# Norm vector folded into two dense weights, more blocks turned by transfers, and a new order of work, in a fused attention and token-mixing kernel

## The chip, the cores and the metric

The kernel runs on one core of a Trainium2 chip. TensorE (PE) multiplies matrices and writes into PSUM; VectorE (DVE) and ScalarE (ACT) compute elementwise and move PSUM to SBUF; GpSimd (POOL) computes elementwise in SBUF and issues the loads; SyncE (SP) issues the stores and the turning transfers. The metric is the device time of one execution in microseconds, as the median of several runs.

## What is computed

```python
kv  = einsum('bhsd,bhse->bhde', k, v)            # 8 batches, 8 heads, 576 tokens, head size 64
o   = einsum('bhsd,bhde->bhse', q, kv)
o   = o / sqrt(mean(o*o, -1) + 1e-6) * g_norm    # g_norm: 64 numbers
x   = o.transpose(0, 2, 1, 3).reshape(8, 576, 512)
theta = x @ w_theta
y   = w_tok_r @ (x*cos(theta)) + w_tok_i @ (x*sin(theta))   # w_tok: 576 x 576, over the tokens
u   = x + y
out = u + maximum(u @ w_ch, 0)
```

All inputs and the output are float32; the kernel computes in fp16 with fp32 sums.

## The kernel before

The 576 tokens of a batch are four full tiles of 128 (j = 0 to 3) and a tail of 64 (j = 4), which is kept with its 512 channels folded onto 128 partitions. For each batch the steps are these; the names are those of the code's tasks, and of the tiles in the profile.

- `ld...`: loads of k, v and q, converted to fp16, from GpSimd's queue.
- `kv`, `ko`: kv of all heads on PE, copied into block-diagonal matrices `kbd` by DVE or ACT.
- `qt`, `qo` or `qd`: the queries turned (transposed). Batches in `TURNED` use a TensorE transpose with an identity and a copy out of PSUM into `qD`; the others use a turning transfer (DMA_TRANSPOSE) from SP into `qDD`, two per batch. The tail always uses TensorE.
- `raw`, `sq`, `ss`, `rt`, `x`: the product with kbd on PE, squares on ACT, row sums on DVE, the power -1/2 on GpSimd, and the scaling on DVE. x is normalized but not yet multiplied by g_norm. One tile `x` holds a pair of token tiles, and both `x` steps of the pair must be done before either is whole.
- `xt`, `xo`: x turned by TensorE into `xps`; the copy out of PSUM multiplies by `gcol` (g_norm along the partitions) and writes `xTb`, of which there are two for all batches (b mod 2).
- `th`, `pt`, `arg`, `abs`, `sin`, `cos`, `z`: theta on PE with `wth`; rounding to whole turns on ACT, the rest on DVE, the absolute value on DVE or ACT, two sines on ACT into `sc`, and the two products with x on DVE into `zm` (tail: `zt`).
- `y`, `ye`: the token mixing on PE, directly in turned form for the full tiles, into `y`.
- `us`: u in turned form on DVE (line 595): y times gcol, plus xTb, into `uTb`. `um`, `ug`, `ute`, `uoe`: the same for the tail, with the factor on GpSimd.
- `ut`, `uo`: u turned back by TensorE into `ups` and copied into `ur`; for batches in `UD` (5 and 6) a turning transfer, `ud`, does it into `urd`.
- `v`, `fin`, `st`: u times `wch` on PE, the maximum and the addition of u on DVE into `ot` (three tiles), and the store on SP.

PSUM has four banks for `acc` (kv, th, y, v), two for `raw` and two for what TensorE turns. SP, like every engine, takes its instructions in order, and one that waits holds those behind it.

Nothing schedules at run time: `plan()` numbers the tasks, and the table `TURNS` is a hand-kept list of these numbers in the order in which they are issued, with a letter where another engine than the planned one takes the step, and with fillers (`f`, `a`, `r`: matmuls on constant data at the start). An engine's program is that list, cut down to its own tasks.

Of the kernel before, what the change touches and what calls it, by code (L numbers as in the profile page):

```python
# [9 lines left out]
FP32 = mybir.dt.float32  # L10
# [8 lines left out]
P = 128  # L19
# [9 lines left out]
NURD = 2  # L29
UD = (5, 6)  # L30
NX, NXE, NUR, NOT, NQD, NQD2 = 4, 3, 3, 3, 4, 4
TURNED = (0, 1)
# [10 lines left out]
def plan():  # L43
# [91 lines left out]
11 17 15 14 0 6 4 1 9 5 2 3 7 8 10 a1 16 f42 51 18 65 f7 43 44 45A 52D 46D f3 53 54 f13 47 48 66 49A  # L135
55 20 f11 58 59D 72 21A 50 f1 60 61 73 12 13 180 177 56 179 178 57 79 67 68 62 80D 69 a1 f8 25 26 63
64 29 70 30A f8 86 22D 87D 71 23A 24 74 37 75 38A 95 76 96D 182 181 77 88 81 33 89 90 82 83 91 34A
452 84 f5 35 31 92 36 93 97 98 78 32D 318 317 320 316 315 319 104 39 105D 85 99 94 100 40 113 327
114 106 27 122 123D 28D 101 107 19 102 115 41 116 108 124 109A 110 125 42A 103 183 184 135 185 217
186 117 118 126 187 127 188D 218 328 119 128 120 111 129 121 134 132 189 196 133 190D 197 191 210  # L140
203 198 112 138 139 130 143 144 192 193 194 140 199 204 211D 200 201 148 195 349 350 145 150 137 205
152 151 714 149 202 206 207 153 131 142 233 224 234 208 448 321 219 322 147 323 481 324 220 326 482D
325A 136 141 225D 209 221 146 222 212 213 214 226 215 223 227 228 229 584 159 447 449 716 450 160
235 164 260 161 166 236 230 261 165 237 216 162 238 163 231 242 251 239 243 252D 262 263 329 167 232
451 253 154 330 240 264 331 244 241 254 155 255 334 169 156 245 613 174 332 581 459 171 335 256A 246
248 257 266 258 336 175 247 157 333 337 712 460 259 158 269 270 273 339 249 250 275 265A 170 267 340
614 338 356 274 268 365 357 279 344 280 345 341 172 284 358 342 453 285 359 366 278 454 283 745 455
343 351 456 360 288 346 367 352 362 347 290 271 353 458D 368 369 370A 457A 173 168 354 746D 291D 348
371 361 363 272 276 383 374 281 277 355 384D 286 364 461 282 392 385 466 287 375 462 393 372 463 289
579 583 964 297 373 302 394 312 464 467 386 468 469 395 298 303 582 376 387 396 313 465 292 294 304  # L150
471 293D 470 488 389 398 397A 377 388A 489 378 305 295 379 580 968 966 842 390 380 399 381 476 299
497 490 391 300 307 382 592 591 296 314 176 306 301 472 308 491 477 401 402 406 473 474 400 492 493A
494 498 478 407 495 479 713 840 411 412 585 405 586 410 416 475 417 587 415 871 588 483 484 589A 499
480 485 872 590D 506 403 486 515 593 496 507D 487 404 500 594 965 598 715 599 516 420 595 501 711
596 408 409 524 502A 503 600 422 525D 423 504 414 413 517 419 418 597 601 838 309 518 519 505 520
602 310 424 439 508 425 509 526 603 426 527 604 440 620 441 608 629 528 621 510 512 311 521 530 723
427 442 511 605 630D 622 429 436 724 443 428 513 514 522 609 534 434 533 523 623 529A 531 610 624
606 532 611 839 837 841 421 539 538 625A 435 430 626 607 437 544 543 717 997 615 718 537 549 612 616
617 548 719 542 720 998 627 849 618 444 547 638 631 721A 722 725 726 632 628 552 554 536 445 619
555D 639D 730 727 633 647 541 640 656 546 553 728 648 731 438 634A 732 729 641 535 850 657 635 735  # L160
733 540 649 736 545 551 642 636 644 734 737 643 761 752 738 550 650 651 753D 645 843 576 844 747 845
658 846 762 748 847A 848 749 739 556 566 431 567 659 557D 637 577 750 740 561 763 432 660 646 652A
741 742 568 558 571 754 764 743 963 967 765 653 654 751 446 433 578 662 661A 562 655 569 570 668 572
788 851 673 744 779 663 789D 559 664 669 790 674 679 755 852 756 758 678 856 853 854 683 573 684 791
780 857 757 792 858 563 855 574 564 859 685 766A 759 781 686 770 767 768 793A 771 794 687 795 860
769 760 976 665 861 670 782 783 772 866 675 667 878 672 862 867 863 560 975 575 864 785 773 784 868
774 680 869 865 666 565 677 671 682 887 676 969 970 873 971 708 776 786 775A 777 681 879 888D 787
# [16 lines left out]
def kernel(  # L184
# [64 lines left out]
    def full(j):  # L249
        return j < NJ  # L250
# [468 lines left out]
```

## Time and profile before

| what | value |
|---|---|
| median of 3 runs | 207.62 us (207.25 to 207.88) |
| the profiled execution | 208.0 us |
| its span, first to last instruction | 206.2 us |
| granted TensorE clock in it | 0.988 |
| busy time PE / DVE / ACT / POOL | 188.1 / 170.7 / 137.2 / 111.1 us |
| bytes moved by DMA | 30.98 MB |

Busy time counts an instruction from start to end; where instructions of an engine overlap, the union is counted. PE's matmuls are pipelined, so a mean of 379 ns for a 512-column matmul is its latency and not the distance to the next one. "Idle before, <- releaser" in a group's row is the time that the engine stood still before these instructions, with what ended it. The chain that ended last is followed back from the last instruction: each piece was released by the one ahead of it.

### The profile page before, as it was taken

To read this page: it belongs to the slowest core of one execution; us is meant where nothing else is said; L and a number is where in the kernel's file an instruction comes from. 1 tells how busy PE (TensorE), PEld (TensorE's weight loads), DVE (VectorE), ACT (ScalarE), POOL (GpSimd) and SP (SyncE) were. 2 spreads that over 40 slices of the span, in tenths; PEclk is the share of its full clock that TensorE was granted. 3 is DMA by queue.
4 is the path that set the end of the run, shared out by engine and by line. 5 is a ranking of instruction groups with operands and counts; after the bars stand their busy time and mean duration, and the time that the engine had idled before them with its cause. 6 is when DMAs were issued, how large, how long until landed. Compare 5 with 4: busy or idle time off the path is not lost.

```text
span 206.2 us, 4614 instructions
## 1 busy us (share of the span) xinstructions
PE 188.1 (91%) x1802; PEld 109.6 (53%) x1802; DVE 170.7 (83%) x346; ACT 137.2 (67%) x276; POOL 111.1 (54%) x112
## 2 busy tenths in 40 slices
PE   0997999999999999999999999979999999999960
PEld 0875766565555555645565756435564554444520
DVE  7036998999999999999998999699998987855560
ACT  2035999369986899767988996959888449500210
POOL 7959984489944985895396534725065320000010
PEclk9999999999999999999999999999999999999995
DMA  5999999999999999899999968919222143236461
GB/s 99 164 197 286 192 190 183 198 164 89 169 189 167 246 184 123 174 155 187 221 151 220 160 154 121 212 24 186 74 105 76 25 80 113 90 77 128 156 244 36
DMA packets 61577, 30.98 MB, mean 150 GB/s; under 512 B 30644, under 2 KB 56884, under 8 KB 61556
## 3 DMA queue, kind: packets, MB, share of 16 engines
q0 software_dynamic: 38864, 16.80, 65.2%
q1 hardware_dynamic: 22692, 13.90, 29.0%
q8 instruction: 14, 0.23, 0.5%
q14 instruction: 7, 0.06, 0.1%
HBM read 33.06 MB, written 9.44 MB: 206 GB/s over the span
## 4 chain that ended last, share of the span: by engine, by line
DVE 34%; PE 32%; DMA 11%; POOL 8%; ACT 6%; issue 6%; DVEq 0%; POOLq 0%
PE y L581 11%; PE th L496 7%; DMA out_dram<-ot 6%; DMA uTb<-in_moe_w_tok_r_dram 5%; DVE zm L556 5%; PE v L496 5%; DVE ot L648 4%; POOL rt L457 4%; DVE uTb L595 4%; DVE ss L451 4%; DVE arg L524 4%; DVE x L469 3%; DVE zt L565 3%; DVE kbd L273 2%; PE xps L388 2%
## 5 line engine op out<-in xcount | busy, mean ns | idle before, releaser
L457 POOL TENSOR_TENSOR rt<-ss,mhalf 128x8 f32<-128x8 f32 x32 | 53.5, 1679 | 44.1 <-DVE ss L451 44.0
L581 PE MATMUL y<-wT,zm 128*128 128x512 f16 x256 | 61.7, 379 | 0.0
L581 PEld LDWEIGHTS <-zm 128*128 128x128 f16 x256 | 23.7, 98 | 24.3 <-issue 0.2
L496 PE MATMUL th<-wth,xTb 128*128 128x512 f16 x128 | 32.7, 379 | 0.1
L496 PE MATMUL v<-wch,uTb 128*128 128x512 f16 x128 | 31.9, 379 | 0.2 <-DVE uTb L595 0.2
L595 DVE SCALAR_TENSOR_TENSOR uTb<-y,gcol,xTb 128x512 f16<-128x512 f32 x32 | 23.2, 741 | 4.4 <-PE y L581 4.4
L269 ACT COPY ur<-ups 128x512 f16<-128x512 f16 x21 | 12.1, 594 | 18.5 <-PE ups L388 18.2
L442 ACT ACTIVATE sqb<-raw 128x512 f32<-128x512 f32 x32 | 19.2, 601 | 7.5 <-PE raw L422 7.4
L469 DVE TENSOR_TENSOR x<-raw,rt 128x512 f16<-128x512 f32 x32 | 21.9, 684 | 2.3 <-POOL rt L457 2.2
L451 DVE TENSOR_REDUCE ss<-sqb 128x8 f32<-128x520 f32 x32 | 21.9, 686 | 2.2 <-ACT sqb L442 1.8
L542 ACT ACTIVATE sc<-arg 128x512 f16<-128x512 f32 x32 | 19.9, 631 | 4.8 <-DVE arg L524 3.9
L548 ACT ACTIVATE sc<-arg,quarter 128x512 f16<-128x512 f32 x32 | 22.8, 724 | 0.1
L524 DVE SCALAR_TENSOR_TENSOR arg<-pt,th 128x512 f32<-128x512 f32 x32 | 21.6, 679 | 1.4 <-ACT pt L519 1.3
L609 POOL TENSOR_TENSOR uge<-ue,g 128x256 f32<-128x256 f16 x8 | 5.4, 673 | 30.5 <-DVE ue L603 30.5
L556 DVE TENSOR_TENSOR zm<-x,sc 128x1024 f16<-128x1024 f16 x32 | 21.5, 681 | 0.1
L519 ACT ACTIVATE pt<-th 128x512 f32<-128x512 f32 x32 | 19.1, 601 | 1.9 <-PE th L496 1.8
L648 DVE SCALAR_TENSOR_TENSOR ot<-v,ur 128x512 f32<-128x512 f32 x24 | 16.1, 681 | 4.5 <-DMA out_dram<-ot 4.0
L496 PEld LDWEIGHTS <-uTb 128*128 128x128 f16 x128 | 11.6, 98 | 11.5 <-issue 0.9
L496 PEld LDWEIGHTS <-xTb 128*128 128x128 f16 x128 | 11.3, 98 | 11.1 <-ACT xTb L271 0.9
L269 ACT CAST kbd<-kv 64x256 f16<-64x256 f32 (+1 forms) x26 | 8.9, 341 | 11.5 <-PE kv L371 11.0
L271 ACT ACTIVATE xTb<-xps,gcol 128x512 f16<-128x512 f16 x20 | 13.6, 684 | 3.5 <-PE xps L388 2.5
L388 PE MATMUL xps<-ident,x 128*128 128x128 f16 x128 | 12.1, 219 | 0.4 <-DVE x L469 0.4
(107 smaller groups left out, 319.5 us busy)
## 6 DMA issues: line engine op xcount, KB each, us to landing
out_dram<-ot SPq DMA_DIRECT2D x32, 256.0 KB, 2.7
k<-in_k_dram POOLq DMA_DIRECT2D x7, 512.0 KB, 11.0
v<-in_v_dram POOLq DMA_DIRECT2D x7, 512.0 KB, 9.1
qh<-in_q_dram POOLq DMA_DIRECT2D x7, 512.0 KB, 10.8
out_dram<-ote SPq DMA_DIRECT2D x8, 128.0 KB
zm<-in_moe_w_theta_dram POOLq DMA_DIRECT2D x1, 768.0 KB, 11.5
uTb<-in_moe_w_tok_r_dram POOLq DMA_DIRECT2D x1, 576.0 KB, 10.3
uTb<-in_moe_w_tok_i_dram POOLq DMA_DIRECT2D x1, 576.0 KB, 12.9
```

What stands on the lines that cost most here:

```text
L269: nc.scalar.copy(out=dst, in_=src)
L451: nc.vector.reduce_sum(out=ss[:], in_=live.pop(("sq", b, j))[:], axis=AXX)
L457: nc.gpsimd.tensor_tensor(out=rt[:], in0=live.pop(("ss", b, j))[:], in1=mhalf[:, 0:h], op=ALU.pow)
L469: nc.vector.tensor_tensor(out=live["xp", b, p][:, :, a * HC:(a + 1) * HC].rearrange("p t (h e) -> p h t e", e=D), in0=r[:].rearrange("p (h ...
L496: nc.tensor.matmul(t[:], lhs(kc), w[:, kc, :], start=(kc == 0), stop=(kc == NKC - 1))
L524: nc.vector.scalar_tensor_tensor(out=arg[:, 0, :], in0=live.pop(("pt", b, j))[:], scalar=MAGIC, in1=live.pop(("th", b, j))[:], op0=ALU.sub ...
L542: nc.scalar.activation(out=sc[:, 1, :], in_=live["arg", b, j][:, 0, :], func=AFT.Sin, bias=0.0, scale=-TURN * SHRINK,)
L548: nc.scalar.activation(out=live["sc", b, j][:, 0, :], in_=live.pop(("arg", b, j))[:, 1, :], func=AFT.Sin, bias=quarter[:], scale=-TURN * S ...
L556: nc.vector.tensor_tensor(out=zm[b % NZ][:, j, :, :], in0=x.unsqueeze(1).broadcast_to((P, 2, C)), in1=sc[:], op=ALU.mult,)
L581: nc.tensor.matmul(t[:], r[:, c * P:(c + 1) * P], wT[:, w, 0:SM], start=(w == 0), stop=(w == 2 * NJ))
L595: nc.vector.scalar_tensor_tensor(out=uTb[:, b % NUT, :, c, :], in0=live.pop(("y", b, c))[:].rearrange("p (j t) -> p j t", j=NJ), scalar=gc ...
L648: nc.vector.scalar_tensor_tensor(out=ot[:], in0=live.pop(("v", b, j))[:], scalar=0.0, in1=u, op0=ALU.max, op1=ALU.add,)
```

## The change

- **The norm vector goes into the weights.** w_theta is scaled row by row with g_norm (it was scaled with a constant in the same step), and w_ch gets a new step `wcs` that scales it in place: three instructions on DVE, one on ACT. So xTb and uTb hold x and u without g_norm: the copies `xo` and `uoe` have no scale any more, and `us` is a plain addition.
- **Where u itself is needed** in the last step, g_norm comes in when u is turned back: `ut` is now an ordinary product with `gdiag`, a diagonal matrix of g_norm, into an fp32 PSUM tile, and `uo` reads fp32.
- **x of batches 5, 6 and 7** (full tiles) is turned by transfers on SP, `xd`, two per batch, straight into xTb. The transposes and copies for them go.
- **u of batches 4, 5 and 6** (before: 5 and 6) is turned back by transfers; since it lacks g_norm, GpSimd multiplies each tile (`um2`, 12 of 128x512, fp32 out, three buffers).
- **Batch 2's queries** are turned by TensorE instead of two transfers.
- **The table `TURNS` is new.** Every line of it differs.

Counted over the program: 48 transposes of x and 16 of u fewer and 16 of queries more on PE; on SP six transfers of x and two of u more and two of queries fewer; 12 products more on GpSimd; full copies of turned x 20 to 13 on ACT and 12 to 7 on DVE.

```diff
-NURD = 2
-UD = (5, 6)
+NURD, NUM2 = 2, 3
+UD = (4, 5, 6)
+XD = (5, 6, 7)
-TURNED = (0, 1)
+TURNED = (0, 1, 2)
...
+    for kc in range(NKC):
+        add("wcs", "DVE", kc)
...
-            add("xt", "PE", b, j)
-            add("xo", "ACT", b, j)
+            if b not in XD or j == NJ:
+                add("xt", "PE", b, j)
+                add("xo", "ACT", b, j)
+            elif j % 2 == 0:
+                add("xd", "SP", b, j // 2)
...
+            if b in UD and j < NJ:
+                add("um2", "POOL", b, j)
...
 TURNS = """
-11 17 15 14 0 6 4 1 9 5 2 3 7 8 10 a1 16 f42 51 18 65 f7 43 44 45A 52D 46D f3 53 54 f13 47 48 66 49A
+8 6 0 9 1 4 5 2 3 17 15 14 16 f28 55 69 20 70D 21 56 7 11 10 r1 83 18 f10 47 48 50D 49A f3 57 58 f17
...
+        nc.vector.tensor_scalar(
+            out=gth[:], in0=gcol[:], scalar1=UNIT / (2.0 * math.pi), scalar2=None, op0=ALU.mult
+        )
+        nc.vector.tensor_scalar(
+            out=gdiag[:], in0=ident[:], scalar1=gcol[:], scalar2=None, op0=ALU.mult
+        )
 
     def e_wth(eng, kc):
-        by = UNIT / (2.0 * math.pi)
-        copy_out(eng, wth[:, kc, :], wth_s[:, kc, :], by)
+        copy_out(eng, wth[:, kc, :], wth_s[:, kc, :], gth[:])
+
+    def e_wcs(eng, kc):
+        copy_out(eng, wch[:, kc, :], wch[:, kc, :], gcol[:])
...
-        copy_out(eng, dst, live.pop(("xp_", b, j))[:], gcol[:])
+        copy_out(eng, dst, live.pop(("xp_", b, j))[:])
+
+    def e_xd(eng, b, p):
+        src = live["xp", b, p][:].rearrange("p t c -> p (t c)")
+        dst = xTb[b % NXT][:, 2 * p:2 * p + 2, :, :].rearrange("p j k c -> p (j k) c")
+        nc.sync.dma_start_transpose(out=dst, in_=src)
...
-        nc.vector.scalar_tensor_tensor(
+        nc.vector.tensor_tensor(
             out=uTb[:, b % NUT, :, c, :],
-            in0=live.pop(("y", b, c))[:].rearrange("p (j t) -> p j t", j=NJ), scalar=gcol[:],
-            in1=xTb[b % NXT][:, :, c, :], op0=ALU.mult, op1=ALU.add,
+            in0=live.pop(("y", b, c))[:].rearrange("p (j t) -> p j t", j=NJ),
+            in1=xTb[b % NXT][:, :, c, :], op=ALU.add,
         )
...
-        copy_out(eng, d[:], live.pop(("up", b, NJ))[:], gcol[:])
+        copy_out(eng, d[:], live.pop(("up", b, NJ))[:])
 
     def e_ut(eng, b, j):
-        turned("ups", lambda i: uTb[:, b % NUT, j, i, :], NKC, ("up", b, j))
+        t = live["up", b, j] = bank([P, NKC, P], FP32, "tr", 2, "ups")
+        for i in range(NKC):
+            nc.tensor.matmul(
+                t[:, i, :], uTb[:, b % NUT, j, i, :], gdiag[:], start=(i == 0), stop=(i == NKC - 1)
+            )
...
+    def e_um2(eng, b, j):
+        u = live["ur", b, j] = wk("um2", [P, C], FP32, NUM2)
+        nc.gpsimd.tensor_tensor(
+            out=u[:].rearrange("p (h e) -> p h e", h=H),
+            in0=live.pop(("ud", b, j)).rearrange("p (h e) -> p h e", h=H),
+            in1=g8[:].unsqueeze(1).broadcast_to((P, H, D)), op=ALU.mult,
+        )
```

Three places show how the instructions move. The first is SP's queue around batch 5. Before, it holds stores (ot full tiles, ote tails) and the turning of batch 6's queries (qDD from qh0):

```order
L654 DMA out_0_dram<-ot_1802 128x512
L654 DMA out_0_dram<-ot_1800 128x512
L412 DMA_TRANSPOSE qDD_1970<-qh0_72 128x8x128
L654 DMA out_0_dram<-ot_1885 128x512
L412 DMA_TRANSPOSE qDD_2071<-qh0_72 128x8x128
L660 DMA out_0_dram<-ote_2018 2x64x256
L654 DMA out_0_dram<-ot_2242 128x512
```

After it, the same part of the queue, with batch 5's x going to xTb1:

```order
L694 DMA out_0_dram<-ote_2069 2x64x256
L688 DMA out_0_dram<-ot_1864 128x512
L515 DMA_TRANSPOSE xTb1_87<-x_2127 128x8x128
L688 DMA out_0_dram<-ot_1922 128x512
L430 DMA_TRANSPOSE qDD_2242<-qh1_73 128x8x128
L515 DMA_TRANSPOSE xTb1_87<-x_2244 128x8x128
L688 DMA out_0_dram<-ot_2341 128x512
L430 DMA_TRANSPOSE qDD_2362<-qh1_73 128x8x128
```

Between the stores of batches 2 and 3 now stand two transfers of x, and batch 7's queries (qh1) in place of batch 6's.

The second is DVE where it makes batch 5's x. Before (x_2062 is the pair of tiles 0 and 1, uTb from xTb1 is batch 3's addition, `L275 ... xTb` the scaled turned copies):

```order
L469 TENSOR_TENSOR x_2062<-raw_1999,rt_2054 128x4x2x64
L595 SCALAR_TENSOR_TENSOR uTb_90<-y_2013,gcol_104,xTb1_87 128x4x128
L524 SCALAR_TENSOR_TENSOR arg_2095<-pt_2064,th_2043 128x512
L469 TENSOR_TENSOR x_2062<-raw_2025,rt_2081 128x4x2x64
L451 TENSOR_REDUCE ss_2101<-sqb1_97 128x8
L534 TENSOR_SCALAR arg_2095<-arg_2095 128x512
L595 SCALAR_TENSOR_TENSOR uTb_90<-y_2066,gcol_104,xTb1_87 128x4x128
L524 SCALAR_TENSOR_TENSOR arg_2119<-pt_2117,th_2087 128x512
L275 TENSOR_SCALAR xTb1_87<-xps_2109,gcol_104 128x512
```

After, where the pair is x_2127:

```order
L487 TENSOR_TENSOR x_2127<-raw_2061,rt_2125 128x4x2x64
L579 TENSOR_TENSOR zm1_81<-x_1741,sc_1932 128x1024
L618 TENSOR_TENSOR uTb_90<-y_2075,xTb1_87 128x4x128
L487 TENSOR_TENSOR x_2127<-raw_2080,rt_2130 128x4x2x64
L618 TENSOR_TENSOR uTb_90<-y_2100,xTb1_87 128x4x128
L469 TENSOR_REDUCE ss_2219<-sqb1_97 128x8
L682 SCALAR_TENSOR_TENSOR ot_2223<-v_2153,ur_1930 128x512
L579 TENSOR_TENSOR zm1_81<-x_1916,sc_2143 128x1024
```

The turned copy is gone, and batch 3's last two additions stand around the pair's second half; xTb1 is free for the transfer after the later of them.

The third is GpSimd's program near its end. Before, batch 7's rt steps and the tails' products (uge):

```order
L457 TENSOR_TENSOR rt_2696<-ss_2694,mhalf_95 128x8
L457 TENSOR_TENSOR rt_2711<-ss_2698,mhalf_95 128x8
L457 TENSOR_TENSOR rt_2803<-ss_2801,mhalf_95 128x8
L609 TENSOR_TENSOR uge_2848<-ue_2755,g8_101 128x256
L457 TENSOR_TENSOR rt_2850<-ss_2829,mhalf_95 128x8
```

After, with the products of batch 4's turned u (um2 from urd):

```order
L665 TENSOR_TENSOR um2_2593<-urd_2500,g8_101 128x512
L475 TENSOR_TENSOR rt_2654<-ss_2650,mhalf_95 128x8
L665 TENSOR_TENSOR um2_2695<-urd_2656,g8_101 128x512
L475 TENSOR_TENSOR rt_2697<-ss_2693,mhalf_95 128x8
L665 TENSOR_TENSOR um2_2757<-urd_2500,g8_101 128x512
L475 TENSOR_TENSOR rt_2759<-ss_2751,mhalf_95 128x8
L475 TENSOR_TENSOR rt_2815<-ss_2811,mhalf_95 128x8
L665 TENSOR_TENSOR um2_2817<-urd_2656,g8_101 128x512
```

Each rt of batch 7's first tiles now stands behind a product that waits for a transfer; the products of batches 5 and 6 follow these, with nothing but tails between them.

More of the change, by code (lines that the diff above doesn't have):

```diff
@@ L140 @@
[L140 to L160, printed above, removed]
@@ L238 @@
     one = const.tile([1, P], FP32, name="one")
+    gth = const.tile([P, 1], FP32, name="gth")
+    gdiag = const.tile([P, P], FP16, name="gdiag")
     gcol = const.tile([P, 1], FP32, name="gcol")
@@ L646, in e_fin @@
         u = live.pop(("ur", b, j) if full(j) else ("ug", b))
-        u = u if b in UD and full(j) else u[:]
         nc.vector.scalar_tensor_tensor(
-            out=ot[:], in0=live.pop(("v", b, j))[:], scalar=0.0, in1=u,
+            out=ot[:], in0=live.pop(("v", b, j))[:], scalar=0.0, in1=u[:],
             op0=ALU.max, op1=ALU.add,
```

69 lines of the change are left out of this document (45 added, 24 removed).

## The prediction

> **What bounds the kernel now.** I read the stretches first: the busy time of each engine in four stretches of the span (the first number after the times is the stretch's length).
>
> ```profile
> core 0: us, PE busy (x) PEld busy (x) DVE busy (x) ACT busy (x) POOL busy (x), PEclk, DMA share, GB/s
> 45.00:90.00 45.00, 43.88 (x428) 24.67 (x425) 43.89 (x86) 37.20 (x76) 34.52 (x35) 1.00 1.26 167
> 90.00:165.00 75.00, 72.48 (x700) 42.01 (x701) 70.69 (x140) 61.90 (x124) 39.08 (x32) 1.00 0.84 137
> 165.00:190.00 25.00, 24.85 (x135) 11.65 (x134) 17.68 (x34) 10.63 (x21) 1.53 (x2) 1.00 0.40 101
> 190.00:206.20 16.20, 9.17 (x73) 4.83 (x71) 7.00 (x13) 1.76 (x3) 0.67 (x1) 0.85 0.37 139
> ```
>
> DVE is busy 43.89 of 45 us from 45 to 90 and 70.69 of 75 from 90 to 165, then falls to 17.68 of 25. PE's busy time is near full everywhere, but it counts pipelined matmuls twice, so its true pace has to come from the chain that ended last: its share by engine, then some of its pieces (start, length, what).
>
> ```profile
> DVE 34%; PE 32%; DMA 11%; POOL 8%; ACT 6%; issue 6%; DVEq 0%; POOLq 0%
> ...
> 89.08 0.48 DVE xTb L275
> 90.04 0.38 PE raw L422 x4
> ...
> 94.53 0.45 PE ups L388 x8
> 106.08 0.44 PE ye L590 x8
> 111.59 0.88 PE th L496 x4
> 112.50 0.60 ACT pt L519
> 117.89 0.42 DVE sse L451
> 123.89 0.68 DVE ot L648
> 124.60 9.54 DMA out_dram<-ot
> ...
> 180.26 8.86 PE y L581 x41
> ```
>
> Eight transposes take 0.45 us, 0.056 each; a 512-column matmul takes 8.86/41 = 0.216; eight ye matmuls take 0.44, 0.055 each. With the code's counts (288 y, 256 th and v of full tiles, 288 transposes of 128x128 and 128 query products of the same shape, 144 ye and 128 tail matmuls) that is 62.2 + 55.3 + 23.3 + 15.0 = 156 us, without the small kv products and the fillers. So two engines share the bound: in the chain DVE stands up to 90, PE from 90 to 112, ACT to 117, DVE again to 165, and PE from there to the last y at 189.
>
> The third thing to see is the 9.54 us of a store at 124.60: DVE had no free output tile (there are three) until it landed. DVE's own waits for stores (total, times, longest), and the page's row of the stores (KB each, median us to landing):
>
> ```profile
> DVE ot L648 <- DMA out_dram<-ot: 4.0, 2, 2.2
> out_dram<-ot SPq DMA_DIRECT2D x32, 256.0 KB, 2.7
> ```
>
> 4.0 us in two waits, the longer 2.2; a store lands 2.7 us after its issue (median of 32).
>
> **The change part by part.** The prices, each row with its count, busy time and mean ns of one:
>
> ```profile
> L388 PE MATMUL ups<-ident,uTb 128*128 128x128 f16 x96 | 8.9, 219 | 0.0
> L422 PE MATMUL raw<-kbd,qD 128*128 128x128 f16 x32 | 3.4, 219 | 1.2 <-DVE x L469 0.8 <-DVE kbd L273 0.2
> L595 DVE SCALAR_TENSOR_TENSOR uTb<-y,gcol,xTb 128x512 f16<-128x512 f32 x32 | 23.2, 741 | 4.4 <-PE y L581 4.4
> L469 DVE TENSOR_TENSOR x<-raw,rt 128x512 f16<-128x512 f32 x32 | 21.9, 684 | 2.3 <-POOL rt L457 2.2
> L275 DVE TENSOR_SCALAR xTb<-xps,gcol 128x512 f16<-128x512 f16 x12 | 5.7, 476 | 0.8 <-PE xps L388 0.6
> L275 DVE TENSOR_SCALAR xTe<-xps,gcol 128x256 f16<-128x256 f16 x4 | 1.4, 344 | 0.3 <-PE xps L388 0.3
> L273 DVE COPY ur<-ups 128x512 f16<-128x512 f16 x3 | 1.2, 414 | 0.4 <-PE ups L388 0.4
> L534 DVE TENSOR_SCALAR arg<-arg 128x512 int32<-128x512 int32 x16 | 7.4, 464 | 0.1
> L271 ACT ACTIVATE xTb<-xps,gcol 128x512 f16<-128x512 f16 x20 | 13.6, 684 | 3.5 <-PE xps L388 2.5 <-DVE uTb L595 0.8
> L269 ACT COPY ur<-ups 128x512 f16<-128x512 f16 x21 | 12.1, 594 | 18.5 <-PE ups L388 18.2 <-DVE ot L648 0.3
> L609 POOL TENSOR_TENSOR uge<-ue,g 128x256 f32<-128x256 f16 x8 | 5.4, 673 | 30.5 <-DVE ue L603 30.5
> ```
>
> PE. 48 transposes of x (batches 5 to 7) and 16 of u (batch 4) leave, 16 of batch 2's queries come: (48 + 16 - 16) x 0.056 = 2.7 us less. By place: 48 leave between 90 and 165 (batches 5 and 6, and u of 4), 2.7 us; 16 leave in the stretch from 165 on, 0.9; 16 come between 45 and 90, 0.9. The remaining 80 transposes of u become products with a diagonal matrix into an fp32 bank. The ordinary product of that shape, raw, has 219 ns, the transpose 219 too: no price, neither way. [...]
>
> DVE from 90 to 165 (batches 3 to 6), counted in the order of both kernels. Before, five full turned copies and three half ones, 5 x 0.476 + 3 x 0.344 = 3.4 us; after, three full ones without the scale, 3 x 0.414 = 1.2: 2.2 less. Two scaled half copies of u's tail go to ACT, at about the 0.344 of the same shape: 0.7 less. Seven full absolute values become five, and a half one goes: about 1.2 less. The addition that makes uTb loses its multiplier, 12 of them here: it costs between 0.684 (the other two-operand form from PSUM) and 0.741 (if the four-piece output makes it slow and not the multiplier); I take 0.684, nearest in form: 0.7 less. One copy of u reads fp32 instead of fp16, between 0.414 and 0.684; I take 0.684: 0.3 more. Sum: 4.5 us less, 3.8 at the worse end.
>
> DVE from 45 to 90: one full turned copy and a half one of x more go than come (0.8 less), one kv eviction and a tail copy less, against three scalings of w_ch (between 0.41 and 0.48 each by the rows of that width), two query copies and one more fp32 copy of u: the sum is 0.3 to 0.5 more. The chain is on DVE there, so I count 0.3; the 0.9 us of transposes that PE gains lie beside it.
>
> ACT loses some 6.5 us over the kernel (20 scaled copies at 0.684 become 13 plain ones at 0.594, 21 copies of u become 15). With 61.90 us of 75 from 90 to 165 it is the lightest of the three, so I count none of it.
>
> GpSimd gets 12 products of 128x512. Between the 0.673 of half the width and twice that, 1.35; I take 1.3, since elements and not instructions dominate uge's row: 16 us on an engine that is busy 1.53 of 25 us from 165 on. Queued behind them are rt of batch 7: the product for tile 1 of batch 4 stands ahead of batch 7's first rt, and needs the first of u's two transfers. Both wait for DVE's last addition of batch 4; DVE has some 13 instructions between that and the ss that rt needs, about 8 us at 0.6 each, and two transfers and a product take about 1.3 + 1.3 + 1.2 + 1.3 = 5. Hidden; without that cover it would be up to 5 us once.
>
> SP gets eight turning transfers more and two fewer. Their price is read here (start, length in SP's queue):
>
> ```profile
> 163.15 2.64 SPq L632 DMA_TRANSPOSE urd<-uTb  x2
> ...
> DMA to landing us min/median/max: 3.1/3.1/3.1
> ```
>
> About 1.3 us each in the queue and 3.1 from issue to landing, against some 1.1 for transpose and copy. What hides the longer way is the order: batch 5's first transfer may go when DVE has added the last piece of batch 3 (they share a buffer), and DVE has 17 instructions, some 10 us, before it needs the angle that PE makes from it; for batch 6 about 14 instructions, some 9 us. If that cover fails, each of the six costs up to 2 us, 12 in all. The first 45 us load the same bytes in nearly the same order, and work there only changes places: nothing, within 1 us either way. The tail from 190 on keeps its eight full tiles and three output tiles: nothing.
>
> Sum: from 90 to 165 both engines get lighter, and the smaller of the two decides, PE's 2.7 us; from 165 on PE's 0.9; from 45 to 90 0.3 more. 2.7 + 0.9 - 0.3 = 3.3 us less. The profiled execution took 208.0 us (span 206.2 and 1.8 around it), 0.4 over the median of 207.62; so 204.7 for it, and 204.3 for the median.
>
> **The rivals.** Gains and losses under 0.3%, 0.6 us, cannot be told from none.
>
> *More than forecast.* DVE's 4.5 us count from 90 to 165, because PE's waits there were made by DVE, and the wait for the late store goes with the new order (its 2.2 of the 4.0 us). Then 4.5 + 0.9 - 0.3 + up to 2.2 = 5 to 7.3 us: 200.3 to 202.6, say 201.5. For it speaks that DVE carries 117 to 165, against it that PE follows so closely.
>
> *No gain.* PE loses its transposes but meets its waits elsewhere: the 2.7 us are filled by waits of the same kind as before, because every place is tied to DVE by the order, and the 0.9 of batch 2's queries counts in full: 3.3 - 2.7 - 0.6 = 0, 207.6, within 0.6.
>
> *Slower: stores stuck behind turning transfers.* SP works in order. Batch 5's first transfer waits for DVE's last addition of batch 3, and behind it stands the store of an output tile that DVE had finished some eight microseconds earlier; the same at batches 6 and 7. With three output tiles DVE comes back for that tile about 12 instructions, 7 us, after the transfer goes. A store of median length (1.3 of the transfer's issue + 2.7 = 4.0) is in time; one as late as the 9.54 us of 124.60 costs 1.3 + 9.5 - 7 = 3.8. Once, it eats the gain (208.1); twice, it makes 211.9. It decides from the second such landing on. For it: the row at 124.60, with loads running; against: in new places fewer loads are left, and the median is 2.7.
>
> *Slower: GpSimd in DVE's way.* In the trace of before one absolute value met a product on GpSimd (start, length):
>
> ```profile
> 68.72 0.66 POOL L609 TENSOR_TENSOR uge<-ue,g 128x256 f32<-128x256 f16 x1
> 68.89 0.77 DVE L534 TENSOR_SCALAR arg<-arg 128x512 int32<-128x512 int32 x1
> ...
> L534 DVE TENSOR_SCALAR arg<-arg x16: 412/420/766, 25.0 to 177.8; 128x512 int32<-128x512 int32 x16
> L556 DVE TENSOR_TENSOR zm<-x,sc x32: 672/680/705, 28.2 to 182.7; 128x1024 f16<-128x1024 f16 x32
> ```
>
> It took 0.77 instead of a median of 0.42: 0.35 lost, until the product ended. The new products are twice as long. If each of the 12 catches one absolute value or one zm for half of its 1.3 us and DVE is on the path, 12 x 0.65 = 7.8 us, 212.1; if the four of batch 4 do (the others come when DVE has room), 2.6 us, 206.9. Slower by over 0.6 us needs six of them on the path: 208.2. Against it: zm's longest is 705 although rt runs most of that time. [...]
>
> **How the numbers follow.** Forecast 0.52, more 0.14, no gain 0.12, stores 0.13, GpSimd 0.09. Faster 0.52 + 0.14 = 0.66, within 0.3% 0.12, slower 0.13 + 0.09 = 0.22. The range goes from 201.0, inside the case of more, over no gain to 208.6, past one late store and the six collisions; outside lie part of the case of more and the repeated mishaps, under 2 in 10. The forecast's own range is 202.6 to 206.0: 1 us for the start and 0.7 for DVE's ends, either way.
>
> **What would show it.** Right: fewer than 100 transposes of x and about 56 ns each for the products with the diagonal; uTb's row near 684; DVE under 67 us of work for what is now 90 to 165; th of batches 5 to 7 without a wait for a transfer; the last y about 3 us before 189. Wrong: waits of PE for xTb transfers in sum over 2 us; DVE's wait for stores over 4.0; zm or the absolute values with means raised by 0.1 us or more.

## The result and the profile after

| | before | after |
|---|---|---|
| median, timed together, 20 runs each | 207.92 us (206.98 to 216.9) | 208.24 us (203.83 to 213.43) |
| ratio, 95% interval | 1 | 0.9861 (0.9824 to 0.9898) |
| the profiled execution / its span | 208.0 / 206.2 us | 206.4 / 204.3 us |
| granted clock in it | 0.988 | 0.982 |
| busy PE / DVE / ACT / POOL | 188.1 / 170.7 / 137.2 / 111.1 us | 187.7 / 171.1 / 132.3 / 125.9 us |

The ratio leaves out every execution that took over 1.5% more than its kernel's fastest, one of the 20 before and eleven of the 20 after (208.23 us and up), so it tells what the change does in an execution that goes well, and not that every one does: the medians over all 20 are level, 207.92 and 208.24. Applied to the 207.62 of the first table it gives 0.9861 x 207.62 = 204.7 us (204.0 to 205.5); the forecast was 204.3.

The two programs do different work at the same time of the clock, so I cut both spans at the same work: where DVE starts the additions that finish batch 0, batch 2 and batch 7 (rows of DVE's timeline: start, length, engine, line, what; in brackets how long the engine stood still before it and for whom). After:

```profile
48.93 0.69 DVE L618 TENSOR_TENSOR uTb<-y,xTb 128x512 f16<-128x512 f32 x1
95.74 1.27 DVE L618 TENSOR_TENSOR uTb<-y,xTb 128x512 f16<-128x512 f32 x2
188.97 1.29 DVE L618 TENSOR_TENSOR uTb<-y,xTb 128x512 f16<-128x512 f32 x2 [1.25 <-PE y L604]
```

Before, the same rows start at 46.08, 92.63 and 189.15. The stretches between them, busy time of each engine in the order PE, PEld, DVE, ACT, POOL, then the granted clock. Before:

```profile
0.00:46.08 46.08, 38.57 (x476) 26.83 (x477) 32.38 (x78) 26.78 (x55) 36.05 (x46) 1.00 1.34 186
46.08:92.63 46.55, 45.60 (x442) 25.75 (x440) 45.31 (x90) 38.35 (x78) 36.35 (x35) 1.00 1.24 167
92.63:189.15 96.52, 93.89 (x813) 51.81 (x812) 85.17 (x168) 70.36 (x142) 37.98 (x31) 1.00 0.73 129
189.15:206.20 17.05, 10.02 (x77) 5.23 (x75) 7.85 (x14) 1.76 (x3) 0.67 (x1) 0.86 0.35 132
```

After:

```profile
0.00:48.93 48.93, 41.66 (x486) 28.87 (x487) 34.01 (x84) 26.94 (x55) 39.43 (x51) 0.97 1.30 176
48.93:95.74 46.81, 46.72 (x463) 27.18 (x461) 45.73 (x91) 41.24 (x88) 33.22 (x30) 1.00 1.26 178
95.74:188.97 93.23, 90.56 (x760) 48.24 (x758) 83.25 (x157) 62.98 (x129) 48.33 (x41) 1.00 0.79 141
188.97:204.30 15.33, 8.76 (x59) 4.41 (x57) 8.08 (x14) 1.17 (x2) 4.94 (x5) 0.88 0.45 156
```

Start +2.85, batches 1 and 2 +0.26, batches 3 to 7 -3.29, end -1.72: together -1.9 us of span. In the long stretch PE stood still 96.52 - 93.89 = 2.63 us before and 93.23 - 90.56 = 2.67 after: its waits are as long as ever, and the stretch shrank by 3.29, nearly the 3.33 us that PE has less to do. DVE lost 1.92 there and ACT 7.38.

The chain that ended last agrees: by engine, from the page of after, where before had DVE 34% and PE 32%.

```profile
PE 62%; DVE 14%; DMA 10%; POOL 4%; ACT 4%; issue 3%; DVEq 0%; SPq 0%; POOLq 0%; ACTq 0%
```

Four of its pieces that do not belong to PE (start, length, what):

```profile
9.98 11.28 DMA zm<-in_moe_w_theta_dram
21.28 0.90 DVE wth L285
...
121.14 6.70 DMA out_dram<-ot
...
170.15 1.38 DVE arg L557
```

The first two are the longer start, the third is a late store again, the fourth is an absolute value that takes three times its usual time. The groups of instructions on which the forecast had a price (count, busy time, mean ns of one):

```profile
L648 PE MATMUL ups<-gdiag,uTb 128*128 128x128 f16 x80 | 7.0, 219 | 0.0
L406 PE MATMUL xps<-ident,x 128*128 128x128 f16 x80 | 7.9, 224 | 0.1
L618 DVE TENSOR_TENSOR uTb<-y,xTb 128x512 f16<-128x512 f32 x32 | 21.0, 683 | 4.0 <-PE y L604 4.0
L283 DVE CAST ur<-ups 128x512 f16<-128x512 f32 x5 | 3.4, 683 | 0.0
L665 POOL TENSOR_TENSOR um<-urd,g 128x512 f32<-128x512 f16 x12 | 14.0, 1177 | 16.8 <-DMA urd<-uTb 15.6 <-DVE ot L682 1.2
L579 DVE TENSOR_TENSOR zm<-x,sc 128x1024 f16<-128x1024 f16 x32 | 22.0, 703 | 1.4 <-ACT sc L571 1.1
L588 DVE TENSOR_TENSOR zt<-xe,sce 64x256 f16<-64x256 f16 x32 | 9.7, 302 | 0.6
L557 DVE TENSOR_SCALAR arg<-arg 128x512 int32<-128x512 int32 x14 | 7.6, 546 | 0.1
```

The upper four are as priced, and GpSimd's product took 1.18 us against the 1.3 counted. The lower three have raised means: before, zm had 681, zt 286 and the absolute value 464.

### The profile page after: what moved, and what is told of

It reads as the page before. It is cut to its first block, busy times and chain, and to the rows that moved or that the text cites. A ratio compares the mean times of both kernels' runs of the same rounds, so it can differ in the third digit from the quotient of the medians.

```text
span 204.3 us, 4547 instructions
## 1 busy us (share of the span) xinstructions
PE 187.7 (92%) x1761; PEld 108.7 (53%) x1761; DVE 171.1 (84%) x344; ACT 132.3 (65%) x272; POOL 125.9 (62%) x124
## 4 chain that ended last, share of the span: by engine, by line
PE 62%; DVE 14%; DMA 10%; POOL 4%; ACT 4%; issue 3%; DVEq 0%; SPq 0%; POOLq 0%; ACTq 0%
PE y L604 25%; PE v L519 10%; PE th L519 9%; DMA zm<-in_moe_w_theta_dram 6%; DMA out_dram<-ot 4%; PE ye L613 4%; DVE arg L547 3%; PE raw L440 3%; PE xps L406 2%; PE kv L389 2%; PE ups L648 2%; DVE zm L579 2%; DVE ot L682 2%; DVE x L487 2%; PE th L526 1%
## 5 line engine op out<-in xcount | busy, mean ns | idle before, releaser
L618 DVE TENSOR_TENSOR uTb<-y,xTb 128x512 f16<-128x512 f32 x32 | 21.0, 683 | 4.0 <-PE y L604 4.0
L665 POOL TENSOR_TENSOR um<-urd,g 128x512 f32<-128x512 f16 x12 | 14.0, 1177 | 16.8 <-DMA urd<-uTb 15.6
L579 DVE TENSOR_TENSOR zm<-x,sc 128x1024 f16<-128x1024 f16 x32 | 22.0, 703 | 1.4 <-ACT sc L571 1.1
L519 PEld LDWEIGHTS <-xTb 128*128 128x128 f16 x128 | 11.8, 101 | 11.4 <-issue 1.8
L279 ACT CAST ur<-ups 128x512 f16<-128x512 f32 x15 | 8.6, 587 | 13.7 <-PE ups L648 13.6
L475 POOL TENSOR_TENSOR rte<-sse,mhalf 128x4 f32<-128x4 f32 x8 | 8.7, 1093 | 11.8 <-DVE sse L469 11.7
L682 DVE SCALAR_TENSOR_TENSOR ot<-v,ur 128x512 f32<-128x512 f32 x20 | 13.5, 685 | 2.7 <-DMA out_dram<-ot 1.1
L279 ACT CAST kbd<-kv 64x256 f16<-64x256 f32 (+1 forms) x28 | 9.8, 350 | 5.4 <-DVE kbd L283 3.9
L555 ACT ACTIVATE arg<-arg 128x512 f32<-128x512 f32 x18 | 11.3, 630 | 1.6 <-DVE arg L547 1.6
```

Source lines behind the costliest of these rows:

```text
L475: nc.gpsimd.tensor_tensor(out=rt[:], in0=live.pop(("ss", b, j))[:], in1=mhalf[:, 0:h], op=ALU.pow)
L519: nc.tensor.matmul(t[:], lhs(kc), w[:, kc, :], start=(kc == 0), stop=(kc == NKC - 1))
L579: nc.vector.tensor_tensor(out=zm[b % NZ][:, j, :, :], in0=x.unsqueeze(1).broadcast_to((P, 2, C)), in1=sc[:], op=ALU.mult,)
L618: nc.vector.tensor_tensor(out=uTb[:, b % NUT, :, c, :], in0=live.pop(("y", b, c))[:].rearrange("p (j t) -> p j t", j=NJ), in1=xTb[b % NXT] ...
```

## The experiments

Ratios are to the kernel before, timed on the same chip and formed as in the section above, with 95% intervals; a run's time is its median. 1% is 2.1 us. Differences between two kernels are worked out from their ratios, the errors added in squares. "Long stretch" is the cut above, from the finishing additions of batch 2 to those of batch 7.

**1. Constant products in PE's idle place at the start.** At the start PE stood still 1.1 us for DVE's copy of a turned w_tok, which stood behind a conversion of w_theta (its tile 3), which waited for its load. Then the granted clock fell (stretches of after):

```profile
20.00:23.00 3.00, 1.64 (x19) 1.34 (x18) 1.92 (x4) 2.51 (x5) 2.66 (x3) 1.00 1.16 203
23.00:26.50 3.50, 3.44 (x19) 1.75 (x20) 1.90 (x5) 1.52 (x3) 2.21 (x2) 0.51 1.48 194
```

```diff
-... 22D 80 37 85 90 101 ...
+... 22D 80 a5 37 85 90 101 ...
```

> The changed kernel with five constant matmuls (5 x 0.216 us) in the place near 21.3 us where PE stood still for 1.3 us; nothing else moves. Theory 'clock': the granted clock of 0.5 from 23.1 to 26.5 us in the changed kernel comes from PE's thin load just before it, and costs about 1.7 us of PE work there; then the clock of this run is 1.0 up to the end, the first th products are 0.86 us apart in fours instead of 1.7, and the time falls by 1.5 to 2.5 us against the changed kernel, to some 0.975 to 0.98 of before, with less spread. Rival 'late weights': the start is late since DVE waits for w_theta at 21.3; then the fillers change under 0.5 us.

Measured: 205.58 us (6 runs), 0.9823 (0.9764 to 0.9883); profiled 204.31 us, full clock, and PE busy 2.77 of the same 3 us:

```profile
20.00:23.00 3.00, 2.77 (x28) 1.96 (x27) 1.75 (x4) 2.33 (x5) 3.00 (x3) 1.00 1.17 209
23.00:26.50 3.50, 3.50 (x37) 2.11 (x35) 2.91 (x7) 2.54 (x6) 1.87 (x3) 1.00 1.48 192
```

Batch 0 was finished at 47.83 instead of 48.93. The difference to the changed kernel, 0.8 us by the ratios, is inside the error of 1.5. And the drop is a matter of the run: of the five other profiles with this very start (3, 4, 5, 6 and 8 below) none shows it, though in run 4 PE waited for the same copy by 0.8 us.

**2. The conversion of w_theta's tile 3 later.** DVE's `wth3` moves behind the copy of w_tok and the first x.

```diff
-... 42A 29 24D 30 75 99 78 23A ...
+... 42A 29 30 75 99 78 24D 23A ...
```

> The changed kernel with DVE's first conversion of w_theta (tile 3) moved behind the copy of wT and the x that stood behind it. Theory 'late weights': wT's copy no longer waits for the weights (1.1 us of DVE's idle time at 21.3), PE's pause at 22.6 goes, the clock stays up, and the time falls by 1 to 2.5 us against the changed kernel, to 0.975 to 0.98 of before. Rival: w_theta's own arrival at 21.3 sets the first th whatever DVE does before; then under 0.5 us.

Measured: 206.17 us (6 runs), 0.9845 (0.9773 to 0.9916); batch 0 finished at 47.34, full clock. The time cannot be told from the changed kernel's. Nor does the place of the conversion explain the start: of the profiles of the changed kernel's own start with a full clock, that of run 5 has batch 0 finished at 46.56 and that of run 8 at 47.39.

**3. x of batches 5 to 7 on PE again**, with its copies on ACT, at the places where the transfers stood:

```diff
-XD = (5, 6, 7)
+XD = ()
```

> The changed kernel with x of batches 5 to 7 turned on PE again (48 transposes, 2.7 us) and copied by ACT (12 copies of 0.59, 7.1 us), at the places of the transfers. Forecast's theory, PE's removed work is the gain: 2.5 to 3.5 us slower than the changed kernel, 0.998 to 1.003 of before. Rival, DVE's lighter load is the gain: DVE is untouched here, so within 1 us of the changed kernel, 0.985 to 0.99 of before.

Measured: 209.48 us (12 runs), 1.0041 (1.0010 to 1.0071): 1.8 points, 3.7 +- 1.0 us, over the changed kernel, and all of its gain gone. The long stretch:

```profile
94.35:192.52 98.17, 93.97 (x808) 51.02 (x806) 83.12 (x158) 69.03 (x141) 48.42 (x41) 1.00 0.64 118
```

PE has 93.97 - 90.56 = 3.4 us more to do, and stands still 4.2 us instead of 2.7; 1.4 of it are waits for ACT's copies, in an order that was not made for them. So this run is an upper bound of what the transposes cost.

**4. No product on GpSimd** for the turned u of batches 4 to 6:

```diff
-        u = live["ur", b, j] = wk("um2", [P, C], FP32, NUM2)
-        nc.gpsimd.tensor_tensor(
...
+        live["ur", b, j] = live.pop(("ud", b, j))
```

> The changed kernel without GpSimd's 12 products: the last addition reads the transfer's output directly (it leaves out the factor g_norm on that u in batches 4 to 6). Theory 'GpSimd in DVE's way': in the changed kernel's trace five DVE instructions beside those products took 2.3 us longer than their kind; if that was on the path, 1.5 to 2.5 us faster than the changed kernel. Rival: DVE had room there and PE sets the end from 150 us on: within 0.5 us.

The kernel leaves out the factor g_norm there. Measured: 205.18 us (6 runs), 0.9815 (0.9756 to 0.9875): 1.0 +- 1.5 us under the changed kernel, unclear as a time. The durations are clear, and the same rows of DVE are back at their old means:

```profile
L579 DVE TENSOR_TENSOR zm<-x,sc 128x1024 f16<-128x1024 f16 x32 | 21.4, 682 | 1.8 <-ACT sc L571 1.6
L588 DVE TENSOR_TENSOR zt<-xe,sce 64x256 f16<-64x256 f16 x32 | 9.2, 286 | 0.6
L557 DVE TENSOR_SCALAR arg<-arg 128x512 int32<-128x512 int32 x14 | 6.3, 457 | 0.1
```

32 x 0.021 + 32 x 0.016 + 14 x 0.089 = 2.4 us of DVE's time go to the products. One such meeting in after, GpSimd's row and then DVE's:

```profile
168.97 3.58 POOL L665 TENSOR_TENSOR um<-urd,g 128x512 f32<-128x512 f16 x3
```

```profile
170.15 1.38 DVE L557 TENSOR_SCALAR arg<-arg 128x512 int32<-128x512 int32 x1
171.46 0.67 DVE L547 SCALAR_TENSOR_TENSOR arg<-pt,th 128x512 f32<-128x512 f32 x1
172.17 0.68 DVE L557 TENSOR_SCALAR arg<-arg 128x512 int32<-128x512 int32 x1
```

The absolute values took 1.38 and 0.68 instead of 0.42; between them the two-input form that reads PSUM took its usual 0.67 beside the same products. The longest zm took 1.27 (median 0.68). In all, 24 of DVE's instructions in after meet a product, and four of them are longer than their kind: these two absolute values, that zm and one zt (0.78), together by 2.3 us; each of the four ends behind the product that it met first. So zm and zt, with two inputs in SBUF, were held by a product, and so was the absolute value, with one, while the form between them, which reads PSUM, was not; nor was the sum of squares that met a product (at 153.71, one input in SBUF, 0.68 against a median of 0.69). What sets these two one-input forms apart, no run shows.

**5. 2.7 us more work on PE alone.** Ahead of each full th of batches 5 to 7 four constant 128x128 products.

```diff
+            for _ in range(NKC if b in XD else 0):
+                nc.tensor.matmul(t[:, 0:P], ident[:], fill[:, 0:P], start=True, stop=True)
```

> The changed kernel with four constant 128x128 matmuls ahead of each full tile of the angle's product in batches 5 to 7: 48 more matmuls of 0.056 us, 2.7 us of work on TensorE and none elsewhere, at the places where the 48 transposes of x stood before. Outputs are unchanged. If TensorE's work sets the end there (the forecast's theory), the time rises by 2 to 3 us over the changed kernel and stands 0.5 to 1.5 us under the kernel before. If the gain of taking the transposes off TensorE came from the copies that left DVE and ACT with them, or from the shorter chain, the matmuls fill TensorE's waits and the time rises by less than 1 us.

Measured: 206.86 us (12 runs), 0.9898 (0.9858 to 0.9937), beside 0.9874 for the changed kernel (run 8): 0.5 +- 1.4 us more. The long stretch took 94.84 us against 93.23, 1.6 more, with a late store in both. By its time this run speaks for waits that take the work in; by its long stretch for PE, as far as one profile of each can tell (that of run 8, the changed kernel again, is at 97.48). It is repeated as 11.

**6. 4.4 us more work on DVE alone.** Ahead of each full sum of squares of batches 3 to 6 a constant fill.

```diff
+        if 3 <= b <= 6 and full(j):
+            nc.vector.memset(spare[:], 0.0)
```

> The changed kernel with one constant fill of 128x256 fp32 on DVE ahead of each full sum of squares in batches 3 to 6: 16 instructions, about 0.27 us each as an estimate, 4.3 us of work on DVE and none elsewhere. Outputs are unchanged. If TensorE's work sets the end from 90 us on, most of this fills DVE's waits, and the time rises by less than 1.5 us. If DVE sets it (the rival in which DVE's 4.5 us count), the time rises by 3 to 4.5 us.

Measured: 206.9 us (12 runs), 0.9945 (0.9902 to 0.9987): 1.5 +- 1.5 us over the changed kernel, for 16 fills of 272 ns. That is the very limit of 1.5 that was set for TensorE, and the error reaches to the 3 set for DVE: it decides nothing. In its profile, besides, the store that DVE waits for in after (121.14) landed after 4.94 us, and DVE did not wait for it, so part of the fills may stand where that wait was. Repeated in another place as 12.

**7. Four output tiles instead of three.**

```diff
-NX, NXE, NUR, NOT, NQD, NQD2 = 4, 3, 3, 3, 4, 4
+NX, NXE, NUR, NOT, NQD, NQD2 = 4, 3, 3, 4, 4, 4
```

The rest of the edit is the narrower filler operand named here:

> The changed kernel with four output tiles of 128x512 instead of three; the room comes from the constant operand of the filler products, which is a quarter as wide and is used four times. If the store that DVE waits for at 121.14 (6.70 us, 1.1 us of DVE's time and 1.33 of TensorE's) is on the path, the time falls by 1 to 1.5 us. If the wait is filled from elsewhere, it changes by less than 0.5 us.

Measured: 204.2 us (6 runs, 202.89 to 206.21), 0.9797 (0.9743 to 0.9852): 1.6 +- 1.6 us under the changed kernel. DVE waits for no store any more. The long stretch took 92.61 us, 0.6 less than in after, although the profiled start had the clock drop again (finished batch 0 at 48.71).

**8. The changed kernel again**, as a measure for 5 to 7.

> The changed kernel as it is, beside the others on the same chip, as the measure for them. By the profiled execution 206.4 us; its repetitions so far run from 203.8 to 213.4. If their spread is a matter of the clock that TensorE is granted and not of the kernel's work, the profiles again show the same busy times on all engines, and the span differs by stretches with a lower clock.

Measured: 206.23 us (6 runs, 204.78 to 208.97), 0.9874 (0.9818 to 0.9930). The expectation, that the spread is one of the clock and not of the work, is wrong. Its profiled execution was the longest of the six, 208.97 us; its start has no clock drop (batch 0 at 47.39), and its long stretch takes 97.48 us. The chain says why: behind the transfer of batch 5's x (SPq L515) a store was issued that took 9.09 us to land, and DVE, and then PE, waited for its tile.

```profile
119.30 0.64 SPq L515
119.94 0.05 issue
119.99 9.09 DMA out_dram<-ot
...
129.17 0.06 DVE ot L682
129.23 0.55 issue
129.78 0.69 DVE x L487
130.47 0.04 issue
130.51 0.59 PE raw L440 x4
```

PE was busy 0.16 of the 3.67 us before 130.50, and here the clock falls behind the pause: 0.56 in the 3.4 us after it.

```profile
126.83:130.50 3.67, 0.16 (x1) 0.00 (x0) 1.33 (x3) 0.60 (x1) 0.00 (x0) 0.94 1.19 164
130.50:133.90 3.40, 3.39 (x31) 2.58 (x31) 2.38 (x5) 1.26 (x3) 1.64 (x1) 0.56 1.17 232
```

The same store is late in six of the seven profiles with this order and three tiles, by different amounts. Landing time and DVE's longest wait for it: 6.26 and 0.5 (run 1), 6.70 and 1.1 (after), 6.79 and 1.2 (run 5), 7.17 and 1.5 (run 2), 8.18 and 2.5 (run 4), 9.09 and 3.4 (run 8). So the wait is the landing time less 5.6 to 5.8, and it differs by 2.9 us between executions. That is one source of the changed kernel's spread; the clock drop at the start is another. That the last two loads (512 KB each, issued 0.3 and 1.2 us behind this store in run 8) make it late is likely: a store lands 2.8 us after its issue in the median, and this one lands, by and large, the sooner, the later the first of the two loads follows it. With three tiles or four, its landing takes 7.6 to 9.1 us where the load is issued 0.1 to 0.3 us behind the store (4, 7, 8, 11), 6.3 to 7.3 at 0.6 to 0.8 (after, 1, 2, 5, 10), and 4.94 at 1.2 (6); in run 12, where the load went 1.6 us ahead, it is 9.09. No run moved the loads on purpose.

**9. The kernel before with four output tiles.** The edit is that of 7.

> The kernel before with four output tiles of 128x512 instead of three (room from a narrower filler operand, as in the run of the changed kernel with four). In its profile DVE waited for stores 4.0 us in two waits. If the kernel before is held by that wait as the changed one is by its own, its time falls by 2 to 4 us, and the gain of the change stays what the engines' work makes of it only against this kernel: the changed kernel with four tiles would be 0 to 2 us faster than this one. If the forecast's theory holds, that the change gains by TensorE's work and the store is covered, the time falls by less than 1 us, and the changed kernel with four tiles stays some 3 us or more faster.

Measured: 207.41 us (12 runs), 0.9955 (0.9920 to 0.9989): 0.9 us faster. The 4.0 us that DVE waited for stores before were thus mostly covered, as was set for the forecast's theory (under 1 us). Its long stretch, and behind it that of run 7:

```profile
93.20:188.76 95.56, 93.41 (x813) 51.80 (x812) 85.43 (x167) 70.52 (x142) 38.06 (x31) 1.00 0.73 130
```

```profile
95.51:188.12 92.61, 90.57 (x760) 48.20 (x758) 83.67 (x157) 63.01 (x129) 48.38 (x41) 1.00 0.81 143
```

With four tiles on both sides the change is worth 0.9797 / 0.9955 = 0.984 (about 0.978 to 0.991), 3.3 us, and in the long stretch 2.95, of which PE's work is 2.84. The gain is not a matter of the stores.

**10 to 12. The edits of 1, 2 and 7 together, alone and with the loads of 5 and of 6.** In 12 the fill stands ahead of each full `fin` and writes half of the output tile, which `fin` then overwrites:

```diff
+        if 3 <= b <= 6 and full(j):
+            nc.vector.memset(ot[:, 0:HC], 0.0)
```

> The changed kernel with the three single edits together: five constant products in TensorE's idle place before 23 us, the last conversion of w_theta behind the first evictions, four output tiles. Start and late store are at different places, so if both theories hold, the gains add: 1 to 1.5 us from the start and 1 to 1.6 from the store, 202 to 203.5 us, and its repetitions lie within 3 us of each other. If the start's gain is given back by the store or later, it is no faster than with four tiles alone.

> The kernel of the three edits with 48 constant 128x128 matmuls more, 2.7 us of work on TensorE in batches 5 to 7. No late store can hide it here. If TensorE alone sets the pace there, the time rises by 2.3 to 3 us over the kernel of the three edits; if DVE does, by less than 0.8; if both take turns, by 1 to 2.

> The kernel of the three edits with a constant fill of half an output tile on DVE ahead of each full last addition in batches 3 to 6: 16 of 0.272 us (the measured length in the run with such fills), 4.4 us of work on DVE. If TensorE alone sets the pace there, the time rises by less than 1 us; if DVE does, by 3.5 to 4.4; if both take turns, by 1.5 to 3.

Measured. Together: 203.81 us (6 runs, 203.13 to 208.06), 0.9771 (0.9727 to 0.9815), faster than both kernels; against the changed one about 2 +- 1.5 us. That is a little short of the 202 to 203.5 expected, and one run of the six lies 5 us over the others. Over the kernel before it is 4.8 us. With PE's load: 205.92 us, 0.9873 (0.9822 to 0.9924), 2.1 +- 1.4 us more for 2.7 us of work. The long stretches, first together, then with PE's load:

```profile
93.98:186.07 92.09, 90.32 (x760) 48.30 (x758) 82.99 (x157) 63.05 (x129) 48.55 (x41) 1.00 0.82 143
```

```profile
94.82:189.13 94.31, 92.75 (x808) 51.00 (x806) 82.99 (x157) 63.67 (x129) 48.84 (x41) 1.00 0.83 141
```

PE's busy time rose by 2.43 and the stretch by 2.22; PE's idle time stayed at 1.6 to 1.8. That lies between the 1 to 2 set for both taking turns and the 2.3 to 3 for PE alone, and the error of 1.4 covers both, and just touches the under 0.8 set for DVE; the stretch is nearest to PE alone.

With DVE's load: 208.79 us (12 runs), 1.0008 (0.9975 to 1.0040), 4.9 +- 1.1 us more, three times the price of run 6. By the limits set this is DVE's case (3.5 to 4.4), against run 11. But the load is not the 4.4 us that was counted. In run 6 the instruction behind a fill starts before the fill has ended, as DVE's instructions mostly do here:

```profile
131.68 0.27 DVE L471 MEMSET spare<- 128x256 f32 x1
131.86 0.64 DVE L472 TENSOR_REDUCE ss<-sqb 128x8 f32<-128x520 f32 x1
```

In run 12 the addition writes the same tile as the fill, and starts only 0.10 us or more after the fill's end:

```profile
146.24 0.27 DVE L684 MEMSET ot<- 128x256 f32 x1
146.62 0.69 DVE L685 SCALAR_TENSOR_TENSOR ot<-v,ur 128x512 f32<-128x512 f32 x1
```

So a fill delays what stands behind it by 0.27 us in run 6, but by 0.46 to 0.51 in run 12, 7.6 us in all. 4.9 of 7.6 is under what a DVE without any room would give, and far over what it would give if it did not matter. Runs 5, 6, 11 and 12 together say that work on either engine is paid at least in part; the errors are too wide to order the two.

The profiled execution of run 12 was its longest, 213.29 us, and is no picture of the median. What it shows is another late landing, that of batch 5's first turning transfer, for which PE waited 3.3 us, and behind it 6.8 us at half clock, from 126.5:

```profile
118.72 9.53 DMA xTb<-x
```

```profile
PE th L520 <- DMA xTb<-x: 3.3, 1, 3.3
```

In run 10 the same transfer cost PE 0.3.

## Why the prediction was right, and where it was not

**PE's work sets the end from 90 us on: right for what was taken away, nearly in size.** It counted 2.7 + 0.9 = 3.6 us less; PE's busy time in the long stretch fell by 3.33 and the stretch by 3.29. With four tiles on both sides it is 2.84 and 2.95. The transposes put back take the whole gain (run 3). Work on PE alone put back, 2.7 us, is paid at 0.5 +- 1.4 us in run 5 and at 2.1 +- 1.4 in run 11, 1.6 and 2.2 by the long stretches; so that all of the gain is PE's work, and none of it the copies and waits that went with it, is likely and not shown. The stretch is PE's busy time plus 1.6 to 3.2 us in ten of the fourteen profiles; it is more only where PE waited for copies in an order not made for them (run 3, 4.2) or for late landings (runs 4, 8 and 12). So the busy time is a fair measure of PE's pace here: it is a union, and does not count pipelined matmuls twice (the last 41 y products of before, of 379 ns each, stand in 8.86 us of its chain), against what the prediction says.

**"The smaller of the two decides": wrong.** In the long stretch DVE's relief was the smaller, 1.92 us against 3.33, and the stretch fell by 3.29. Nor is DVE out of the matter: fills on it cost 1.5 us in one place and 4.9 in another. The forecast gave DVE 4.5 us of relief from 90 to 165, with DVE under 67 us of work there as its mark; 70.69 - 1.92 = 68.8 misses it. Without the products on GpSimd it would be 85.17 - 81.17 = 4.0, by this row of run 4:

```profile
94.95:188.99 94.04, 90.30 (x760) 48.29 (x758) 81.17 (x158) 62.90 (x129) 39.57 (x33) 1.00 0.80 142
```

So the count was good, and the term that was missing is the rival's: GpSimd takes 2.1 us of it back. Its price in time, by run 4, is 1.0 +- 1.5 us, or nothing that can be told. The rival in which DVE's whole relief counts is thereby answered as far as its size goes: there was not that much.

**From 45 to 90, +0.3: right in size, by luck.** It is +0.26, though a little later by the clock; and in ten other profiles with this order of batches 1 and 2 the stretch is 46.8 us as in after. But the forecast kept the chain on DVE there and let PE's 0.9 us lie beside it. In after PE is busy 46.72 of the 46.81 us and the chain that ended last runs on PE alone through this stretch; before, it stood on DVE for over half of it, and PE had 0.95 us to spare. So it was PE's 1.12 us more that used this up and lengthened the stretch.

**The start, "nothing, within 1 us either way": wrong.** By the finish of batch 0 it takes 46.56 to 48.93 us in the twelve profiles with the changed start, against 46.08 and 46.66 in the two of the kernel before. From the first product of th on there is no difference: 23.7 us in the two of before, 23.7 to 24.1 in eleven of the twelve, and 25.0 in after, with its spell at half clock. The loss is made ahead of it. That product starts at 22.4 and 23.0 us before, whether w_theta's load had landed at 21.3 or at 20.5; with the changed start it comes at 22.7 to 25.0, always 1.7 to 2.8 us behind that landing (20.5 to 22.3). The step that failed is "work there only changes places". In after, and in runs 5 and 8, the chain goes from that load over a conversion and a copy of w_tok on DVE to the first th, where the chain of before does not touch the load. But with that conversion moved (run 2) it is still 1.7 us and batch 0 is finished at 47.34: what costs the rest stays open.

**The tail, "nothing": wrong, by 1.7 in the other direction.** The forecast looked at the number of tiles and not at the order: before, DVE's addition for the tail of u stood at 196.17, behind five full tiles and a wait of 1.76 for a store, and the half tile ended the kernel from 199.57; in after the tail's half tile starts at 195.74 and three full ones come last, the last at 198.16. The store is the smaller part of it: with four tiles and no such wait (run 9) the kernel before still takes 16.7 us there, and every profile of the changed order but run 12's 15.2 to 15.4. The start's loss and the tail's gain work against each other, which is why the time came out near the forecast by more than its own terms: that part is luck.

**Stores behind turning transfers: the mechanism is there, at the place named.** In after DVE had written the tile at 108.0 us (from 107.33, 0.69 long), and its store was issued at 121.14, right behind the transfer of batch 5's x, which SP issued from 119.40 on. The forecast's formula for the price (1.3 + landing - 7, so landing less 5.7) is what the six landings show, 5.6 to 5.8. Only the landing was taken too well for the forecast (the median of 2.7), and as 9.54 for the rival; it is 6.3 to 9.1 in these six. It happens once and not twice, so it takes part of the gain in some executions, and the point from which it would decide was not reached.

**The single marks.** 80 transposes of x (fewer than 100), 219 ns for the products with the diagonal as for the transposes they replace, 683 for uTb, 0.2 us of waiting for xTb in after, and 1.1 of DVE's for stores: as written. The last y at 188.8 and not 186, because of the start. The mean of the absolute values rose by 0.08, nearly the 0.1 that was set as the mark against the forecast.

## What to carry to other kernels

Cut the two traces at the same work and not at the same time, and compare each stretch's length with each engine's busy time: the engine whose busy time moves with the length, at a constant remainder, is a candidate for setting the pace, and loads put back test it, if their size is read from the trace: a fill of 0.27 us cost 0.27 in one place and nearly 0.5 in another, where the next instruction wrote the same tile. A start and a tail that "only change places" need their waits counted like the middle. Where few buffers stand behind a store, as the three tiles here, its landing time is part of the path (6.3 to 9.1 us, for which DVE waited 0.5 to 3.4), and its spread is then part of the spread of the kernel.

## What the runs showed of the hardware

- The granted clock fell to a half for one spell of some 3.4 us in three profiles, and for 6.8 us in a fourth: in after from 23 us, behind a pause of PE of 1.1 us in a stretch where PE was busy 1.64 of 3; in run 7 from about 17 us, where PE had been busy 1.65 of 3 and 1.08 of 2; in run 8 behind a pause of 3.7 us; in run 12 from 126.5 us, some 1.5 us into PE's wait of 3.3 for the late transfer. A pause of 1.2 us at 128 in after, where PE was busy 1.83 of 3, brought none. In after the spell lasts 3.41 us, from 23.08 to 26.49, and the clock's next change, at 200.57, comes 51 such lengths later. Cut from the changes into pieces of that length, the clock's record in before and after (from 10.32 and 9.43 us on) has 111 of them at full clock, and three were followed by half clock: PE was busy 0.60 of the piece in the first case above (after, from 19.67), and 0.40 (before, from 198.06) and 0.17 (after, from 197.16) where its work ended. In each of the 108 others it was busy 0.63 or more.
- A turning transfer from SBUF to SBUF, 3.1 us from issue to landing in the trace of before, took 9.53 in run 12, at the place where stores took 6.3 to 9.1.
- In after 12 products on GpSimd (128x512, fp16 times fp32, 1.18 us each) held DVE's instructions with two inputs in SBUF (zm 0.68 to 1.27 us, zt 0.29 to 0.78) and the absolute value (0.42 to 1.38); the 20 others that met a product, which read PSUM or a single input in SBUF, kept their usual lengths.
